# Storing the first chunk's x^T earlier, and transposing the keys of two more pieces on VectorE

## The chip, the cores and the metric

The kernel runs on one core of a Trainium2 chip. The core has five engines with a queue of instructions each: TensorE (matrix products; PE in the profile, its weight loads PEld), VectorE (DVE), ScalarE (ACT), GpSimd (POOL) and SyncE (SP), which here issues nearly all DMAs. All transfers share 16 DMA engines. The metric is the device time of one execution in microseconds; of several executions the median counts.

## The reference

A causal linear attention with decay (8 batches, 8 heads, 576 tokens, head size 64), whose output is laid out as 4608 tokens by 512 features, and then a two-layer network with an activation of its own:

```python
gamma = 1.0 - 2.0 ** (-5.0 - np.arange(H))
Dmat = np.where(rel >= 0, gamma[:, None, None] ** rel[None, :, :], 0.0)   # rel = i - j
attn = np.matmul(scale * np.matmul(q, k.transpose(0, 1, 3, 2)) * Dmat, v)
x = attn.transpose(0, 2, 1, 3).reshape(B * S, H * D)      # 4608 x 512
h = x @ w_in                                              # 512 x 2048
g = h * erf(softplus(h))
out = g @ w_out                                           # 2048 x 512
```

Everything is float32.

## The kernel before

**Attention by pieces.** The tokens are cut into 36 pieces of 128 tokens, 9 to a pair of batches: four of the first batch, four of the second, and one that holds the last 64 tokens of both. Pieces are counted from 0 here, so the eleventh and twelfth are pieces 10 and 11. Four pieces make a chunk of 512 tokens, nine chunks in all. Of each piece three stages are run, in an order that the list `stages` (L430 to L435) fixes:

- `transposes(i)` (L311) brings queries and keys into the layout with the head dimension on partitions (tiles qT and kT).
- `scores(i)` (L337) multiplies kT and qT (16 products at L343 into two PSUM tiles s), and VectorE masks them into sT (L348, recorded at the helper's line L99).
- `outputs(i)` (L350) multiplies sT with the values (L361) and the running state with qT (L372), adds k^T v of the piece to the state (L384, and L423 for the decay), and VectorE scales the result into the chunk's x^T (`scaled`, recorded at L99). At its end it loads keys and values of piece i + 3 and, from piece 7 on, has GpSimd weigh the values of piece i + 1 (`weigh_values`, L309).

There are two ways to transpose. For an early piece the rows are loaded as they are (`load_rows`, L136, issues at L145); TensorE transposes them against an identity into PSUM (L328: pt_q, pt_k, four blocks of 128x128 each) and ScalarE copies the result out (L330, L334). For a late piece `load_squares` (L123, issues at L131) loads them in another arrangement, four DMAs of 112 KB for a whole piece, and VectorE transposes squares of 32 by 32 straight into qT or kT (L322). Queries go the second way from piece 8 on (`SQUARES`), keys from piece 12 on (`SQUARES_K`), for the pieces that lie in one batch and for the shared ones alike. Keys that come as squares are loaded as rows as well where a piece lies in one batch, because L384 needs them so. Rows have four buffers for k and v; squares have two for qs and two for ks. `transposes(i)` asks for the queries of piece i + 2 at its end, and with them for the square keys.

**The network by blocks.** The hidden features are cut into four groups g; a block is one group and one chunk. Both products use a scheme with seven products of half size for eight, so blocks need sums of weights and of x^T. `First` makes h of a block (L492), the activation follows (L555 to L569), `Second` the block's share of the output (L600). Block (0, 0) and (0, 1) use plain products instead (`plain`, L535, products at L546). For the groups after the first, x^T is read back from the DRAM tile xd, in which `store_x(c)` (L460) puts it: 1 MB for a chunk, one DMA at L461. Chunk 0 is needed from xd only when group 1 begins.

**The order.** It is written out by hand. TensorE, VectorE and the others run their own instructions strictly in the order of the program. Attention is woven in between the products: up to the first block's activation the string at L723 says step by step what is issued (L723 to L739). Its letters: `a` one stage of the attention, `p` one step of the plain products, `s` the store of chunk 0, `w` a load of weights, `c` the second part of the constants, `k` idle products, a digit that many steps of rounding the weights (L250 to L271, on ScalarE, VectorE and GpSimd). After the string come the store of chunk 1 (L744) and the plain products of block (0, 1).

SyncE's queue issues in the program's order as well. The eight semaphores of its DMAs are used in turn, so each DMA waits until the one eight places before it has landed, besides the waits for its buffer.

Of the kernel before, what the change touches and what calls it, by code (L numbers as in the profile page):

```python
# [54 lines left out]
def kernel(  # L55
# [56 lines left out]
    PC = TCH // P  # L112
# [4 lines left out]


    SQUARES = 2 * PC
    SQUARES_K = 3 * PC  # L120
    SQ = 32

    def load_squares(i, name, src):  # L123
        t = raw.tile([P, NP, P * D // SQ], FP32, tag=name + "s", name=f"raw_{name}s", bufs=2)
        for b, s0, n, r0 in pieces[i]:
            m = n // SQ * D
            for part in range(P // SQ):
                e, d0 = part // 2, part % 2 * SQ
                tokens = src[b, e * NP : (e + 1) * NP, s0 : s0 + n, :].rearrange("p (r a) d -> r p (a d)", r=SQ)
                at = r0 // SQ * D  # L130
                nc.sync.dma_start(  # L131
                    out=t[part * SQ : (part + 1) * SQ, :, at : at + m - SQ], in_=tokens[:, :, d0 : d0 + m - SQ]
                )
        return t

    def load_rows(i, name, src, bufs):  # L136
        if name == "q":
            t = raw.tile([P, NP, P * D // SQ], FP32, tag="qs", name="raw_q", bufs=bufs)
            t = t.rearrange("p a x -> p (a x)")[:, : H * D].rearrange("p (h d) -> p h d", h=H)
        else:  # L140
            t = raw.tile([P, H, D], FP32, tag=name, name=f"raw_{name}", bufs=bufs)
        for b, s0, n, r0 in pieces[i]:
            for e in range(2):
                heads = src[b, e * NP : (e + 1) * NP, s0 : s0 + n, :]
                nc.sync.dma_start(out=t[r0 : r0 + n, e::2, :], in_=heads.rearrange("h p d -> p h d"))  # L145
        return t

    def load(i, names="qkv"):
        if i < len(pieces):
            t = loaded.setdefault(i, {})  # L150
            for name in names:
                src = {"q": q, "k": k, "v": v}[name]
                if name == "q" and i < SQUARES:
                    t["q"] = load_rows(i, "q", q, 2)
                elif name == "q":
                    t["qs"] = load_squares(i, "q", q)
                    if i >= SQUARES_K:
                        t["ks"] = load_squares(i, "k", k)
                elif name == "v" or i < SQUARES_K or len(pieces[i]) == 1:
                    t[name] = load_rows(i, name, src, 4)  # L160
# [67 lines left out]
    def load_weights():  # L228
        part = next(coming, None)
        if part is not None:  # L230
            t = wraw.tile([P, 2 * WP], UINT32, tag="wraw", name="wraw")
            for rows, src in part[0]:
                nc.sync.dma_start(out=t[rows].rearrange("p (h f) -> p h f", h=2), in_=src)
            words.append((t, *part[1:]))
# [49 lines left out]
    def round_weights(n=1):  # L284
        for _ in range(n):
            next(round_step, None)
# [159 lines left out]
    def attend(upto):  # L446
        while done[0] < min(upto, len(stages)):
            of, i = stages[done[0]]
            of(i)
            done[0] += 1  # L450
# [9 lines left out]
    def store_x(c):  # L460
        nc.sync.dma_start(out=xd[c], in_=x[0, c][:, :n_dc])  # L461
# [242 lines left out]
    def keep_busy(n):  # L704
        for _ in range(n):
            nc.tensor.matmul(idle[:, :P], lhsT=ident, rhs=ident, start=True, stop=True)
# [13 lines left out]

    for what in "alkakakawkakakawaa3awwa2aaa5ppappawwppa5ppapp5wawcppa5ppappaa5s":  # L723
        if what == "a":
            attend(done[0] + 1)
        elif what == "p":
            next(products)
        elif what == "s":
            store_x(0)
        elif what == "l":  # L730
            load(2, "kv")
        elif what == "c":
            nc.sync.dma_start(out=cst[:, CONST_FIRST:], in_=consts[:, CONST_FIRST:])
        elif what == "w":
            load_weights()
        elif what == "k":
            keep_busy(2)
        else:
            round_weights(int(what))  # L739
# [92 lines left out]
```

## Time and profile before

| | |
|---|---|
| median of 5 runs | 1028.24 us (1026.79 to 1029.47) |
| the profiled execution's own time | 1028.24 us |
| its span on the core | 1026.5 us |
| TensorE busy | 1017.3 us (99%), 6346 products |
| VectorE busy | 668.6 us (65%) |
| ScalarE busy | 390.6 us (38%) |
| GpSimd busy | 122.6 us (12%) |
| DMA | 165.76 MB, 161 GB/s on average |
| SyncE's loads of queries as squares, L131 | 96 of 112 KB, 4.5 us to landing |
| SyncE's loads of keys as squares, L131 | 84 of 112 KB, 4.2 us to landing |
| stores of x^T, L461 | 9 of 1 MB, 5.3 us to landing |
| transposition of kT on VectorE, L322 | 27, 1102 ns at the median |
| transposition of keys on TensorE, L328 | 48 blocks of 128x128, 12 copies of 588 ns on ScalarE |

Busy time is the union of an engine's instructions; TensorE's products overlap, so the duration of one (272 ns for a block of a transposition) is longer than the step from one to the next. The chain of work is the view that gives each piece of time to one engine, followed back from the last instruction. Times on the axis are microseconds from the start of the span.

### The profile page before, as it was taken

How to read it: one execution, taken by the hardware profiler on the slowest of the kernel's cores; microseconds unless marked ns; L12 is line 12 of the kernel's file. 1: busy time of each engine (PE TensorE's matmuls, PEld its weight loads, DVE VectorE, ACT ScalarE, POOL GpSimd, SP SyncE). 2: the span in 40 equal slices, each digit the busy share in tenths (PEclk: the TensorE clock that was granted, in tenths of full speed). 3: DMA queues.
4: the chain of work that ended last, by engine and by line, in shares of the span. 5: the costliest groups of instructions: out<-in, count | busy, mean ns of one | idle time of the engine just before them, and what ended most of it. 6: DMA issues, size and time to landing. Idle time of an engine off the chain costs nothing.

```text
span 1026.5 us, 15946 instructions
## 1 busy us (share of the span) xinstructions
PE 1017.3 (99%) x6346; PEld 876.4 (85%) x6346; DVE 668.6 (65%) x1054; ACT 390.6 (38%) x481; POOL 122.6 (12%) x122
## 2 busy tenths in 40 slices
PE   9999999999999999999999999999999999999998
PEld 8778888888788888888888888888888888888887
DVE  3868777877976656656666666666567655555555
ACT  2354134233234444434343344444433333333332
POOL 2243112122312110010001001000100000000000
PEclk9999999999999999999999999999999999999999
DMA  9998989979974344544445345444433334444433
GB/s 194 205 247 175 224 194 228 248 149 251 241 179 165 125 145 146 168 161 160 156 147 170 123 146 157 167 146 144 144 124 124 123 131 126 131 136 133 124 92 114
DMA packets 146986, 165.76 MB, mean 161 GB/s; under 512 B 97376, under 2 KB 121568, under 8 KB 138848
## 3 DMA queue, kind: packets, MB, share of 16 engines
q1 hardware_dynamic: 145904, 163.96, 56.6%
q8 instruction: 50, 0.82, 0.3%
q10 hardware_dynamic: 1008, 0.79, 0.3%
q14 instruction: 24, 0.20, 0.1%
HBM read 117.52 MB, written 47.19 MB: 160 GB/s over the span
## 4 chain that ended last, share of the span: by engine, by line
PE 94%; SPq 2%; DMA 2%; DVE 1%; issue 1%; POOL 0%; POOLq 0%; DVEq 0%
PE a L600 24%; PE a L492 23%; PE g L600 12%; PE g L492 12%; PE e L600 6%; PE e L492 6%; PE s L343 3%; PE o L361 3%; DMA raw_v<-in_v_dram 2%; PE o L384 1%; PE o L372 1%; SPq L145 1%; PE p L546 1%; PE pg L546 1%; PE pe L546 1%
## 5 line engine op out<-in xcount | busy, mean ns | idle before, releaser
L492 PE MATMUL a<-x,wa 128*128 128x256 f32 x1088 | 258.3, 380 | 0.0
L492 PEld LDWEIGHTS a<-x,wa 128*128 128x128 f32 x1088 | 205.7, 190 | 28.5
L600 PE MATMUL a<-wb,s 128*128 128x256 f32 x864 | 205.7, 381 | 0.0
L600 PEld LDWEIGHTS a<-wb,s 128*128 128x128 f32 x864 | 162.9, 190 | 23.6 <-ACT o L614 0.7
L99 DVE TENSOR_TENSOR t<-g,t 128x512 f32<-128x512 f32 x68 | 46.9, 690 | 150.3 <-ACT t L522 113.1
L492 PE MATMUL g<-x,wa 128*128 128x256 f32 x544 | 129.2, 380 | 0.0
L492 PEld LDWEIGHTS g<-x,wa 128*128 128x128 f32 x544 | 102.8, 190 | 14.4
L99 DVE TENSOR_TENSOR o<-a,o 128x512 f32<-128x512 f32 x108 | 74.2, 687 | 49.3 <-PE a L600 49.3
L517 ACT COPY t<-a 128x512 f32<-128x512 f32 x34 | 19.9, 586 | 188.2 <-PE a L492 188.2
L99 DVE TENSOR_TENSOR t<-t,s 128x1024 f32<-128x1024 f32 x72 | 88.6, 1271 | 0.0
L561 ACT ACTIVATE s<-t 128x1024 f32<-128x1024 f32 x72 | 72.1, 1048 | 27.6 <-DVE t L99 27.6
L270 POOL TENSOR_TENSOR wraw<-wraw 128x512 f32<-128x512 f32 x28 | 29.4, 1051 | 437.7 <-DVE wraw L268 185.7
L99 DVE TENSOR_TENSOR x<-x 128x512 f32<-128x512 f32 x115 | 75.8, 693 | 1.2
L528 ACT COPY t<-a 128x512 f32<-128x512 f32 x34 | 19.9, 587 | 144.3 <-PE a L492 144.3
L565 ACT ACTIVATE s<-s 128x1024 f32<-128x1024 f32 x72 | 72.1, 1049 | 0.4
L600 PE MATMUL g<-wb,s 128*128 128x256 f32 x288 | 68.6, 381 | 0.0
L600 PE MATMUL e<-wb,t 128*128 128x256 f32 x288 | 68.5, 380 | 0.0
L600 PE MATMUL a<-wb,t 128*128 128x256 f32 x288 | 68.5, 380 | 0.0
L600 PE MATMUL g<-wb,t 128*128 128x256 f32 x288 | 68.2, 380 | 0.0
L99 DVE TENSOR_TENSOR sT<-s,cst 128x512 f32<-128x512 f32 x72 | 46.1, 681 | 32.6 <-PE s L343 32.6
L99 DVE TENSOR_TENSOR o<-g,o 128x512 f32<-128x512 f32 x72 | 49.3, 685 | 24.8 <-ACT o L614 20.0
L492 PE MATMUL e<-x,wa 128*128 128x256 f32 x272 | 64.8, 381 | 0.0
(75 smaller groups left out, 1226.5 us busy)
## 6 DMA issues: line engine op xcount, KB each, us to landing
od<-o SPq DMA_DIRECT2D x54, 512.0 KB, 3.4
x<-xd SPq DMA_DIRECT2D x27, 1024.0 KB, 4.8
o<-od SPq DMA_DIRECT2D x27, 1024.0 KB, 5.6
raw_qs<-in_q_dram SPq DMA_DIRECT2D x96, 112.0 KB, 4.5
raw_ks<-in_k_dram SPq DMA_DIRECT2D x84, 112.0 KB, 4.2
xd<-x SPq DMA_DIRECT2D x9, 1024.0 KB, 5.3
raw_k<-in_k_dram SPq DMA_DIRECT2D x64, 128.0 KB, 4.5
raw_v<-in_v_dram SPq DMA_DIRECT2D x64, 128.0 KB, 4.4
```

Source lines behind the costliest of these rows:

```text
L99: nc.vector.tensor_tensor(out=out, in0=in0, in1=in1, op=op)
L145: nc.sync.dma_start(out=t[r0 : r0 + n, e::2, :], in_=heads.rearrange("h p d -> p h d"))
L270: engine.tensor_tensor(out=r_f, in0=high_f, in1=r_f, op=ALU.mult)
L343: nc.tensor.matmul(ps[e][:, p, :], lhsT=t["kT"][heads[e], p, :], rhs=t["qT"][heads[e], p, :], start=True, stop=True)
L361: nc.tensor.matmul(o[p % 2][heads[(e + p) % 2], p // 2, :], lhsT=t["v"][:, 2 * p + e, :], rhs=t["sT"][:, e, p, :], start=(p < 2), stop=(no ...
L492: nc.tensor.matmul(acc[:, j * TH : (j + 1) * TH], lhsT=weights["wa", self.g][:, a, d, j * P : (j + 1) * P], rhs=x[self.g, self.c][a][:, d, :],
L517: nc.scalar.copy(out=self.t1[:, 1], in_=self.a)
L528: nc.scalar.copy(out=self.t2[:, 0], in_=self.a)
L546: nc.tensor.matmul(acc[n][:, j * TH : (j + 1) * TH], lhsT=wa[:, slots[f], dc % 2, j * P : (j + 1) * P], rhs=t[:, dc, tok * TH : (tok + 1) ...
L561: nc.scalar.activation(self.s[:, j], t, AF.Softplus)
L565: nc.scalar.activation(self.s[:, j], self.s[:, j], AF.Erf)
L600: nc.tensor.matmul(acc[:, tp, :], lhsT=left[:, j * TH + tp * P : j * TH + (tp + 1) * P], rhs=weights["wb", self.g][:, b, j, :], start=(sta ...
```

## The change

Two edits. `SQUARES_K` goes from 12 to 10: the keys of pieces 10 and 11 are loaded as squares too (eight more DMAs; the rows are still loaded) and transposed by VectorE (two more instructions at L322), in place of eight transpositions on TensorE and two copies on ScalarE. And the letter `s` of the string moves from its end to the front of its last stretch: the store of chunk 0 is issued before four steps of products, three stages of attention and five steps of rounding instead of after them. In SyncE's queue it thereby moves ahead of the transfers that these three stages issue: the queries of piece 9 (four DMAs at L131), its keys (two at L145) and its values (two at L145). Later in the queue, the four DMAs of square keys of piece 10 come right behind the square queries of piece 10, and those of piece 11 behind the queries of piece 11.

```diff
-    SQUARES_K = 3 * PC
+    SQUARES_K = 3 * PC - 2
...
-    for what in "alkakakawkakakawaa3awwa2aaa5ppappawwppa5ppapp5wawcppa5ppappaa5s":
+    for what in "alkakakawkakakawaa3awwa2aaa5ppappawwppa5ppapp5wawcppa5sppappaa5":
```

The instructions of GpSimd stay the same, in the same order.

## The prediction

> **What bounds the kernel now.** The first view is the table of stretches, around the place that the diff touches (the store of the first x^T and the transposes of two pieces lie between 57 and 90 us).
>
> ```profile
> core 0: us, PE busy (x) PEld busy (x) DVE busy (x) ACT busy (x) POOL busy (x), PEclk, DMA share, GB/s
> 60.00:80.00 20.00, 20.00 (x206) 16.50 (x204) 14.97 (x29) 8.04 (x12) 7.28 (x7) 1.00 1.08 250
> 80.00:100.00 20.00, 20.00 (x205) 16.36 (x202) 16.86 (x28) 10.59 (x13) 5.71 (x5) 1.00 0.77 170
> 100.00:110.00 10.00, 10.00 (x94) 8.15 (x94) 9.93 (x14) 1.17 (x2) 2.06 (x2) 1.00 0.93 256
> ```
>
> TensorE has no idle time here, and the list of waits shows one real wait of it after 60 us (0.6 us, for kT near 272). So whatever leaves or enters TensorE's own order moves the end one for one. Two other resources are nearly full: the DMA engines at 60 to 80 us (share 1.08) and VectorE at 80 to 110 us.
>
> The second view is the chain that ended last, 66 to 87 us. It runs on TensorE alone and prices what the change removes.
>
> ```profile
> 66.34 1.06 PE pg L546 x4
> 67.41 0.86 PE p L546 x4
> 68.27 0.44 PE pt_k L328 x4
> 68.71 0.86 PE p L546 x4
> ...
> 76.16 0.86 PE pe L546 x4
> 77.02 0.44 PE pt_k L328 x4
> 77.46 0.87 PE pg L546 x4
> ...
> 84.75 1.73 PE a L600 x8
> 86.48 0.44 PE pt_k L328 x4
> 86.92 1.73 PE e L600 x8
> ```
>
> The blocks at 77.02 and 86.48 are the keys of pieces 10 and 11, counted from 0: the two that move to VectorE. The block at 68.27 is piece 9, which stays.
>
> The third view is SyncE's queue, in order of time.
>
> ```profile
> 56.76 0.43 SPq L733 DMA_DIRECT2D cst<-in_decays_dram  x1
> 57.28 2.62 SPq L131 DMA_DIRECT2D raw_qs<-in_q_dram  x4
> 59.95 0.98 SPq L145 DMA_DIRECT2D raw_k<-in_k_dram  x2
> 61.57 1.61 SPq L145 DMA_DIRECT2D raw_v<-in_v_dram  x2
> 63.31 1.13 SPq L461 DMA_DIRECT2D xd<-x  x1
> ```
>
> The qs, k and v here belong to piece 9. From issue to landing the view by tile gives 5.4 us for k, 4.0 for the second v and 6.1 for the 1 MB store: k lands at 60.4 + 5.4 = 65.8, v at 62.8 + 4.0 = 66.8, the store at 63.3 + 6.1 = 69.4. They land in the order of issue, the store 2.6 us behind v.
>
> The fourth is VectorE's timeline around piece 11.
>
> ```profile
> 91.60 2.44 DVE L99 TENSOR_TENSOR wa<-wa 128x512 f32<-128x512 f32 x2
> 93.97 1.27 DVE L99 TENSOR_TENSOR sT<-s,cst 128x512 f32<-128x512 f32 x2
> 95.16 0.69 DVE L322 STREAM_TRANSPOSE qT<-raw_qs 128x512 f32<-128x512 f32 x1
> 95.79 1.11 DVE L322 STREAM_TRANSPOSE kT<-raw_ks 128x512 f32<-128x512 f32 x1
> 98.20 0.69 DVE L99 TENSOR_TENSOR o<-g,o 128x512 f32<-128x512 f32 x1 [1.31 <-ACT o L614]
> ```
>
> sT of piece 11 is ready at 95.24; TensorE uses it at 97.48 (L361). That is 2.24 us of cover. From sT of piece 9 at 75.13 to the end of kT at 96.90 VectorE idles once, 1.17 us at 83 to 84.18, and that for GpSimd's wb, which itself waited for VectorE's L268. So whatever is inserted after 75.13 arrives undiminished at 93.97.
>
> **What the Trainium skill says.** "DMA: Bandwidth & Descriptors", Queues, rings and completion order: each DMA engine consumes its descriptors in ring order. The landings above agree (65.8, 66.8, 69.4), so a store that is issued earlier pushes back all that now comes behind it. "TensorEngine Tiling (Array Packing)", Key Properties: a change of tiling mode drains TensorE. The trace agrees: eight products take 1.92 us right after a group with 64-row weights and 1.73 otherwise; both removed blocks stand between full-size products, so no drain goes with them. "SBUF — State Buffer", SBUF: two separate sides: a VectorE instruction with two SBUF inputs and a GpSimd one exclude each other. The pair wa at 91.60 took 2.44 us beside GpSimd's weighing of v (92.00, 1.49 us), the pair at 88.65 took 1.37.
>
> **The change, part by part.**
>
> *Removed from TensorE:* 2 x 4 transposes, 2 x 0.44 = 0.88 us, on the path, nothing hides it. Gain 0.88. With them go two copies of 0.59 us on ScalarE, which idled 7.1 us before the first: worth nothing. Two fewer PSUM tiles of "at" are taken; the four then turn as they do from piece 12 on, where TensorE never waits for one: nothing.
>
> *Store moved.* It now stands behind the constants (56.76), ahead of three transfers of piece 9: four issues of qs, two of k, two of v. It depends on nothing late (its x^T is complete after piece 3), so it goes at about 57.3. Everything behind it slides by its transfer, 2.6 us by the landings. k of piece 9: 65.8 + 2.6 = 68.4. TensorE begins to load it as weights at 67.89, and with the 0.13 us that GpSimd took between v's landing (66.84) and its start (66.97) the load begins at 68.55. This is a new wait of 0.66 us in front of everything on TensorE. The cover was 67.89 - 65.84 = 2.05 us, which is just too little. Bounds: 0 if engines that were idle behind v at 63 to 65 us take the store faster; 1.75 if it costs 3.6 us, the stretch in which the 1 MB passed (64.3 to 68, at 200 to 370 GB/s). By conservation it can't be much worse, since the same bytes were through at 69.4 before. I take 0.66. qs of piece 9 lands at 65.0 + 2.6 = 67.6, used on VectorE at 68.22: hidden. v lands near 69.5 instead of 66.8, so GpSimd's weighing starts 2.6 us later; GpSimd has nothing else until 73.38 and TensorE needs v at 79.12: hidden. From k of piece 10 on, the bytes ahead are the same as before: no change.
>
> *Added transfers.* Eight DMAs of 112 KB, about 0.55 us apart by their kind's landings: 4.4 us. The square keys of piece 10 take the places in the queue that the square queries of piece 11 hold now, the last of which is issued at 75.03 and lands at 79.6. VectorE wants them after qT, at 80.24: covered by 0.6 us, and by 0.9 more until TensorE would wait (it needs kT at 82.5 - 0.44 = 82.1, so the keys at 81.1; an earlier wait of TensorE adds to this). All behind them slides by 2.2, then 4.4 us: square keys of piece 11 about 84 (needed 89.7), k and v of piece 11 from 81.4 to 86 (needed 92.0), queries and keys of piece 12 by 90 (needed 95.2). The DMA engines are free at 80 to 82 and 83 to 84 us, so the slide is gone by about 92. Eight more issues of 0.43 us on SyncE lie in the same wait. All hidden: nothing.
>
> *Added on VectorE:* two transpositions of kT at 1.08 to 1.14 us each, of which 0.92 (124.39 to 125.31) to 1.11 counts because instructions overlap: 1.0 each. The first stands ahead of L263 and L268, so wb on GpSimd and VectorE's wait for it slide with it. s of piece 10 needs kT at 82.1 and gets it at 81.3 (plus the same 0.66 both): hidden. With the second, sT of piece 11 ends at 95.24 + 2.0 = 97.24, while TensorE would arrive at 97.48 - 0.88 = 96.60; the 0.66 us shift both. The wait is 0.6 us (0.2 of it already at piece 10: 87.9 against 87.7). Bounds: 0 if wa at 91.6 no longer meets GpSimd and gets back 1.07 us; 0.95 at 1.13 each. After that VectorE is led again by TensorE's outputs at 99.24: sT of piece 12 ended at 105.42 and was used at 106.38, so the lag left over, up to 0.4 us, fits: nothing more.
>
> *Sum:* -0.88 + 0.66 + 0.6 = +0.4 us. The profiled execution took 1028.24 us (span 1026.5 and 1.7 around it), which is the median of the five runs too (1026.79 to 1029.47). Forecast 1028.6, 0.04% slower; by the 0.2% (2.06 us) that a measurement of this kernel tells from none, no change.
>
> **Rivals.**
>
> *The gain arrives, 1027.0.* k lands in time and VectorE gets its port back: -0.88. If also the wait of 0.6 us near 272 closes, -1.5: 1026.7. For it: the two lower bounds are possible. Against: the queue is full exactly where the store goes in. To be faster by over 2.06 us it would need more idle time than TensorE has after 57 us, so this rival, too, stays inside 0.2%, apart from the spread of runs.
>
> *k of piece 9 comes much later, 1031.0.* The store would have to cost k over 4.4 us, a landing after 70.2: its stragglers (the constants landed 6.0 us after their issue, most of their packets long before) would hold back k by the store's 3.6 us and a late second issue of k, which waits for the landing of the weights issued at 56.34 (61.5). With 3.0 us of wait: -0.88 + 3.0 + 0.6 = +2.7. It decides from a wait of 2.35 us on. Against: 69.4, when the same bytes were through.
>
> *VectorE becomes the bound to 110 us, 1030.3.* 9.93 of 10 us are busy at 100 to 110. Without any cover, 2.2 + 0.66 - 0.88 = +2.0, at the very edge. Against: the idle 1.31 + 0.34 us at 97 to 99.
>
> *The square keys of piece 10 come late, 1031.* They would have to land after 81.1 (81.8 with the 0.66) instead of 79.6; each us past that costs one, 2 us late gives 1030.6, 2.4 gives 1031.0. For it: they are asked for only at 73 to 75, in the fullest stretch. Against: in the same place of the queue other rows of the same size landed at 79.6.
>
> **How the numbers follow.** The sum near zero, with both waits between their bounds: 0.52, and the gain in full: 0.20, both within 0.2% but for 0.08 (spread of runs and what I didn't see) that I give to faster and 0.02 to slower. k much later 0.10, VectorE as the bound 0.09, square keys late 0.09, of which 0.10 together end inside the 0.2% and 0.18 beyond it. So faster 0.08, within 0.2% 0.72, slower 0.20. The range, 1026.6 to 1031.0, takes in the gain in full and the late k; beyond it I leave 0.08 below and 0.10 above.
>
> **What would show it.** Right: pt_k only up to 68.5 us, eight transposes fewer; a wait of TensorE for raw_k there, 0.3 to 1.2 us; the store issued at 57.3 and landed near 65.5; kT from raw_ks 29 times, the first near 81; no wait for raw_ks longer than 0.5 us; a wait of o (L361) for sT near 97, about half a us. Wrong: TensorE idle over 2 us in one place between 68 and 110, or no wait at all and the span shorter by 0.9.

## The result, and the profile after

| | before | after |
|---|---|---|
| median | 1028.24 us, 49 runs | 1029.53 us, 28 runs |
| lowest and highest | 1026.79, 1029.82 | 1026.90, 1033.49 |
| the profiled execution, its span | 1028.24, 1026.5 us | 1029.54, 1027.8 us |

The ratio of the times is 1.0015, with a 95% interval of 1.0009 to 1.0020: the change costs 1.5 us (0.9 to 2.1). The means of the runs lie 1.5 us apart, the medians 1.3. That is within 0.2% and inside the range, on the side that the forecast named, but 1.1 us more than its +0.4. The highest run moved up by 3.7 us, the lowest hardly at all.

The table of stretches after the change, with one short stretch more (the columns are those of before):

```profile
core 0: us, PE busy (x) PEld busy (x) DVE busy (x) ACT busy (x) POOL busy (x), PEclk, DMA share, GB/s
60.00:80.00 20.00, 19.06 (x190) 15.34 (x187) 14.52 (x26) 6.96 (x10) 8.07 (x7) 1.00 1.13 278
80.00:100.00 20.00, 20.00 (x205) 16.26 (x201) 18.75 (x30) 10.12 (x13) 5.71 (x5) 1.00 1.04 200
100.00:110.00 10.00, 10.00 (x95) 8.19 (x94) 9.93 (x14) 1.17 (x2) 2.06 (x2) 1.00 0.90 249
66.00:70.00 4.00, 3.06 (x16) 2.46 (x16) 3.94 (x7) 0.61 (x2) 0.07 (x1) 1.00 1.35 212
```

TensorE, without a gap here before, now lacks 0.94 us, all of it at 66 to 70. VectorE has 1.9 us more at 80 to 100 (18.75 for 16.86), the two transpositions. The DMA share at 80 to 100 went from 0.77 to 1.04.

The chain that ended last, 63 to 87 us:

```profile
63.66 4.93 DMA raw_k<-in_k_dram
68.59 0.14 issue
68.73 0.63 PE pt_k L328 x4
69.36 0.86 PE p L546 x4
...
76.81 0.86 PE pe L546 x4
77.67 0.86 PE pg L546 x4
...
84.97 1.73 PE a L600 x8
86.69 1.73 PE e L600 x8
```

It no longer runs on TensorE alone. It comes from the keys of piece 9, issued at 63.66 and landed at 68.59; TensorE follows 0.14 us later. Between pe and pg, and between a and e, the two blocks of transposes are gone.

SyncE's queue:

```profile
56.61 1.72 SPq L233 DMA_DIRECT2D wraw<-in_moe_w_out_dram  x1
58.38 0.43 SPq L733 DMA_DIRECT2D cst<-in_decays_dram  x1
58.86 0.43 SPq L461 DMA_DIRECT2D xd<-x  x1
59.38 3.69 SPq L131 DMA_DIRECT2D raw_qs<-in_q_dram  x4
63.12 1.21 SPq L145 DMA_DIRECT2D raw_k<-in_k_dram  x2
64.43 1.24 SPq L145 DMA_DIRECT2D raw_v<-in_v_dram  x2
```

The store stands behind the constants and ahead of piece 9, as planned. But the constants themselves are issued at 58.38, not at 56.76, because the load of weights in front of them held the queue for 1.72 us in this execution, and for 0.38 before.

VectorE's timeline around piece 11:

```profile
94.06 2.44 DVE L99 TENSOR_TENSOR wa<-wa 128x512 f32<-128x512 f32 x2
96.42 1.28 DVE L99 TENSOR_TENSOR sT<-s,cst 128x512 f32<-128x512 f32 x2
97.62 0.70 DVE L322 STREAM_TRANSPOSE qT<-raw_qs 128x512 f32<-128x512 f32 x1
98.25 1.07 DVE L322 STREAM_TRANSPOSE kT<-raw_ks 128x512 f32<-128x512 f32 x1
```

sT comes 2.45 us later than before (96.42 for 93.97). The idle time of 1.31 us in front of the next instruction is used up, and wa still takes 2.44 us. TensorE pays for it in the products of sT (TensorE's timeline, the outputs of pieces 10 and 11), before:

```profile
88.58 1.09 PE L361 MATMUL o<-sT,raw_v 128*64 128x128 f32 x16
...
97.48 1.09 PE L361 MATMUL o<-sT,raw_v 128*64 128x128 f32 x16
```

and after:

```profile
88.35 1.26 PE L361 MATMUL o<-sT,raw_v 128*64 128x128 f32 x16
...
97.42 1.42 PE L361 MATMUL o<-sT,raw_v 128*64 128x128 f32 x16
```

The group of 16 products took 1.09 us for either piece; it now takes 1.26 for piece 10 and 1.42 for piece 11. It is stretched rather than preceded by an idle time: that of piece 11 starts at 97.42, when the second of the two instructions that write sT has not ended.

Last, TensorE's lines in the list of waits (total, times, longest, in us), before:

```profile
PE s L343 <- DVE kT L322: 0.6, 1, 0.6
PE pt_k L328 <- DMA raw_k<-in_k_dram: 0.2, 1, 0.2
```

and after:

```profile
PE s L343 <- DVE kT L322: 1.6, 2, 0.9
PE pt_k L328 <- DMA raw_k<-in_k_dram: 1.5, 2, 0.9
```

The second line holds the predicted wait, its longest, 0.94 us; the other 0.5 us lie ahead of 20 us. In the first there is one that was not predicted, at 234.78 (timeline of VectorE and TensorE); the other, near 273, was there before:

```profile
233.53 1.10 DVE L322 STREAM_TRANSPOSE kT<-raw_ks 128x512 f32<-128x512 f32 x1 [1.38 <-DMA raw_ks<-in_k_dram]
...
234.78 1.16 PE L343 MATMUL s<-qT,kT 64*128 64x128 f32 x16 [0.94 <-DVE kT L322]
```

If each TensorE instruction's start is subtracted from that of the same instruction before, the difference is -0.48 us from 33 us on (waits of the start-up that were shorter in this execution), +0.65 behind the wait at 68, +0.21 and -0.22 behind the two removed blocks, -0.06 and +0.27 behind the outputs of pieces 10 and 11, and +1.3 from 235 us to the end. The spans differ by 1.3. So two questions were left: what does the store cost, and does the wait at 234 belong to the added transfers?

### The profile page after: what moved, and what is told of

Its sections match the earlier page's. It is cut to its first block, busy times and chain, and to the rows that moved or that the text cites. A ratio compares the mean times of both kernels' runs of the same rounds, so it can differ in the third digit from the quotient of the medians.

```text
span 1027.8 us, 15940 instructions
## 1 busy us (share of the span) xinstructions
PE 1016.6 (99%) x6338; PEld 875.0 (85%) x6338; DVE 672.5 (65%) x1056; ACT 389.5 (38%) x479; POOL 124.0 (12%) x122
## 4 chain that ended last, share of the span: by engine, by line
PE 88%; DMA 5%; SPq 2%; DVE 2%; POOL 1%; ACT 1%; issue 1%; DVEq 0%; POOLq 0%
PE a L600 23%; PE a L492 22%; PE g L600 12%; PE g L492 11%; PE e L600 6%; PE e L492 5%; PE s L343 2%; PE o L361 2%; DMA raw_v<-in_v_dram 2%; DMA raw_ks<-in_k_dram 1%; DMA wraw<-in_moe_w_in_dram 1%; PE o L384 1%; PE o L372 1%; SPq L131 1%; SPq L145 1%; PE p L546 1%
```

## The experiments

All ratios are to the kernel before, timed beside them on the same chip. Not all rows come from one chip, so the ratios are to be compared, not the medians.

| kernel | median us | ratio, 95% interval |
|---|---|---|
| store moved only | 1028.65 | 1.0015 (1.0008 to 1.0023) |
| keys only, store at its old place | 1028.04 | 1.0005 (0.9997 to 1.0013) |
| added transfers only, unread | 1028.95 | 1.0010 (1.0002 to 1.0018) |
| change, store still earlier | 1027.98 | 1.0005 (0.9997 to 1.0013) |
| change, store behind the keys of piece 9 | 1028.44 | 1.0009 (1.0002 to 1.0015) |
| added transpositions on VectorE only | 1027.72 | 1.0002 (0.9993 to 1.0010) |
| keys without added transfers | 1027.84 | 0.9998 (0.9990 to 1.0007) |
| TensorE's part only | 1026.85 | 0.9993 (0.9986 to 0.9999) |
| square keys of piece 11 only | 1027.18 | 0.9995 (0.9987 to 1.0003) |

**The store alone.** Only the letter `s` moves.

```diff
-    for what in "alkakakawkakakawaa3awwa2aaa5ppappawwppa5ppapp5wawcppa5ppappaa5s":
+    for what in "alkakakawkakakawaa3awwa2aaa5ppappawwppa5ppapp5wawcppa5sppappaa5":
```

> Only the store moves; the keys of pieces 10 and 11 stay with TensorE. Theory (the store holds back the keys of piece 9, and nothing else of the change costs more than it gives): TensorE waits about 1 us for raw_k at 68 to 69 us, no later wait is new, all that follows is 0.7 to 1.1 us later than before: ratio 1.0007 to 1.0011. Rival (the store is hidden, all the loss is from the keys): no wait for raw_k near 68, ratio 1.000.

It costs 1.5 us (0.8 to 2.4), as much as the whole change and more than the 0.7 to 1.1 expected. TensorE's timeline:

```profile
69.68 0.63 PE L328 MATMUL pt_k<-ident,raw_k 128*128 128x128 f32 x4 [1.43 <-DMA raw_k<-in_k_dram]
```

The wait is there without the key edit, and longer than in the changed kernel. Behind it TensorE is 1.61 us later than before, and it was level in front of it.

**The keys alone.**

```diff
-    SQUARES_K = 3 * PC
+    SQUARES_K = 3 * PC - 2
```

> Only the keys of pieces 10 and 11 move to VectorE; the store stays behind the transfers of piece 9. Theory: no wait for raw_k at 68; TensorE is 0.88 us ahead after 87 us, gives back 0.6 us in waits for sT at 88 and 97 and stands 0.3 us ahead at 100 us. Then two ways: if the eight added transfers keep the queue late until 230 us, TensorE waits about 1 us there for kT and the ratio is 1.0005 to 1.001; if that late wait in the changed kernel's profile was chance, the ratio is 0.9995 to 1.000. Rival (the store is not the cause, the keys are all of it): ratio 1.0015.

+0.5 us (-0.3 to 1.3), no measurable difference. In its profile TensorE gains 0.44 us at each of the two blocks that are gone and gives back 0.28 at 89.6 and 0.32 at 98.5; there is no wait near 68 or 233.

**The key edit taken apart.** Three kernels: only the added DMAs, whose data nobody reads; only two transpositions more on VectorE, into a tile that nobody reads; and the move from TensorE to VectorE without the DMAs, the keys of pieces 10 and 11 being transposed from the squares of the queries.

```diff
 # added transfers only
+                    elif i >= SQUARES_K - 2:
+                        load_squares(i, "k", k)
 # transpositions only
+        if i in (10, 11):
+            extra = att.tile([P, NP, P], FP32, tag="extra", name="extra", bufs=1)
+            squares = t["qs"].rearrange("p h (a d) -> p h a d", d=D)
+            nc.vector.transpose(out=extra.rearrange("p h (r a) -> p h a r", r=SQ), in_=squares[:, :, :, :SQ])
 # without added transfers
+            if i in (10, 11) and name == "k":
+                t["ks"] = t["qs"]
```

> The kernel before, with the square keys of pieces 10 and 11 loaded in their place of the queue but read by nobody: eight more DMAs of 112 KB, no instruction of another engine differs. If added bytes keep the queue late up to 230 us, the loads stand 1 to 1.5 us later there and TensorE waits 0.5 to 1.0 us for kT near 233: ratio 1.0005 to 1.001. If the queue catches up at 125 to 140 us, where it is half idle, no wait of TensorE is new and the ratio is 1.000.

> The kernel before with one more transposition on VectorE at piece 10 and one at piece 11, of data that are there anyway and into a tile that nobody reads; TensorE keeps its own transpositions, and no transfer is added. Theory (the two cost only where TensorE has been moved ahead of them): sT of piece 11 ends near 97.2 instead of 95.2 and TensorE uses it at 97.5: no wait, ratio 1.000, at most 1.0003. Rival (VectorE is the bound up to 110 us): 1 to 2 us of waits between 88 and 111 us, ratio 1.001 to 1.002.

> Keys of pieces 10 and 11 as in the change, transposed by VectorE and not by TensorE, but out of the square queries that are there anyway: no transfer is added, and the store stays where it was (the keys of these two pieces are thereby wrong values). It is the keys' half of the change without its eight DMAs. Theory: TensorE 0.88 us ahead at 87 us, 0.3 us ahead at 100 us after two waits for sT, and nothing new later: ratio 0.9997, range 0.999 to 1.0002; the difference to the same with the transfers (1.0005) is theirs. Rival (the transfers cost nothing, the loss lies in VectorE's order): ratio as with the transfers, 1.0005.

Transfers that nobody reads cost 1.0 us (0.2 to 1.8). By SyncE's queue, landings are 4.4 us later than before at 86 us and still 3.0 at 111; the slide is down to 0.4 only at 133. (Of this, 1.1 us were there at 77, ahead of the first added transfer. In a second execution, shown below, landings were 0.65 us sooner than before at 77, 3.9 later at 87 and 0.9 later at 111.) TensorE's loss in this profiled execution lies at 233 to 273 (two waits for kT, 1.1 us in sum, and a late sT).

The transpositions alone cost nothing that shows (+0.2 us, -0.7 to +1.0). Timelines of VectorE and TensorE (the added lines make L361 L365):

```profile
96.01 1.27 DVE L99 TENSOR_TENSOR sT<-s,cst 128x512 f32<-128x512 f32 x2
...
97.65 1.09 PE L365 MATMUL o<-sT,raw_v 128*64 128x128 f32 x16
```

sT ends at 97.28; TensorE comes at 97.65 and its group keeps the 1.09 us. With TensorE's own transposes still there, the cover of 2.24 us holds the 2.0. Without them and without the DMAs (the third kernel) the group takes 1.41 us again, and TensorE gives back 0.19 at 89 and 0.32 at 98; the time is that of the kernel before (-0.2 us, -1.0 to +0.7). So VectorE's price is paid only because TensorE arrives 0.88 sooner.

**TensorE's part alone.** The transposition of the keys of pieces 10 and 11 is left out on all engines; their scores use kT of piece 9.

```diff
+            if i in (10, 11) and name == "k":
+                t["kT"] = nine[0]
+                continue
...
+            if i == 9 and name == "k":
+                nine.append(tT)
```

> The kernel before with the eight transpositions of the keys of pieces 10 and 11 and their two copies left out; these pieces take kT of piece 9, so no work replaces them. It is the gain of the change by itself. Theory (what leaves TensorE's order moves the end one for one): TensorE stands 0.44 us ahead from 77 us and 0.88 us from 87 us on, no wait for sT at 88 and 97, ratio 0.9991. Rival (later waits, for transfers or for VectorE between 230 and 275 us, take the gain back): ratio 0.9995 to 1.000, with the lead gone behind such a wait.

-0.7 us (-1.4 to -0.1). In the profile TensorE gains 0.43 and 0.44 at the two places and no wait follows. The predicted gain is real and arrives at the end when nothing else is added.

**The store at other places.** Both kernels contain the key edit; in the first the store goes in front of the queries of piece 8, in the second between the keys and the values of piece 9.

```diff
 # still earlier
+    for what in "alkakakawkakakawaa3awwa2aaa5ppappawwppa5ppapp5wsawcppa5ppappaa5":
 # behind the keys of piece 9
-        load(i + 3, "kv")
+        load(i + 3, "k")
+        if i == 6:
+            store_x(0)
+        load(i + 3, "v")
```

> The changed kernel with the store of chunk 0 a stretch earlier still, ahead of the square queries of piece 8 (near 52 us instead of 59), where the DMA engines are half idle (share 0.45 to 0.6 at 50 to 52 us). Theory: part of the store's 2.6 us falls into that idle time, the keys of piece 9 land near 67 and TensorE waits 0 to 0.4 us for them instead of 0.9; against the changed kernel 0.6 to 1.1 us are gained: ratio to before 1.0003 to 1.001. Rival (the store costs the same wherever it stands ahead of piece 9): ratio as the changed kernel's, 1.0015.

> The changed kernel with the store of chunk 0 between the keys and the values of piece 9: the same DMAs, the store one place (two DMAs of values) earlier than in the kernel before, and the values of piece 9 alone behind it. Theory (the store costs by making the keys of piece 9 late, and only by that): no wait for raw_k near 68, TensorE's lead at 77 and 87 us as with the keys' half alone, the values later by 2 to 3 us without a wait of TensorE; ratio 1.0005, as the keys' half alone, 0.001 below the changed kernel. Rival (the store costs by its bytes in a full stretch, wherever it stands ahead): some of the wait stays, ratio 1.001 to 1.0015.

The first is at +0.5 us (-0.3 to 1.3), the value of the key edit alone, with a wait of 0.33 us left on TensorE, as the theory had it; the interval overlaps that of the change, so a gain over it is not shown. In the second the wait is gone (TensorE's timeline):

```profile
67.61 0.60 PE L328 MATMUL pt_k<-ident,raw_k 128*128 128x128 f32 x4
```

Yet its time, +0.9 us (0.2 to 1.5), is not shown to be better than that of the change: the intervals overlap, and it lies between what the theory and the rival gave. Its profiled execution was 1.4 us faster than its median, so what held up the others is not in that trace.

**Half of the keys.** Only piece 11 goes to VectorE.

```diff
-    SQUARES_K = 3 * PC
+    SQUARES_K = 3 * PC - 1
```

> The keys of piece 11 alone move to VectorE, with four more DMAs; the store stays where it was. A half of the change that could beat both kernels: TensorE gains 0.44 us, sT of piece 11 ends at 96.2 when TensorE arrives at 97.0, so that nothing is given back there; half the added transfers. Theory: ratio 0.9995 to 1.0002, as the late waits for transfers grow by half of what eight DMAs cost. Rival (they grow with any added transfer): 1.0005.

-0.5 us (-1.3 to +0.3): the lowest of the versions that leave nothing out, but not distinguished from the kernel before.

**Second executions.** Does the wait after 230 us belong to a kernel, or to one execution of it? The change, the added transfers alone and the kernel before once more, unaltered, one execution each (1028.77, 1027.12 and 1027.88 us).

> The change itself in a second execution, to see which of its waits belong to it. Theory: the wait for raw_k of piece 9 near 68 us comes back, 0.5 to 1.7 us, because the store's transfer in front of those keys is there in every execution; and TensorE waits again between 230 and 275 us, for kT or sT that came late through the transfers, 0.5 us or more in sum. Rival: the waits of the first profiled execution after 230 us were that execution's own; then TensorE loses less than 0.3 us there, and the span is 1.0 us shorter than the first one's 1027.8.

> The kernel before with the square keys of pieces 10 and 11 loaded and left unread, a second execution. Theory: the added transfers cost by waits of TensorE at 230 to 275 us, in sum 1.0 us more than in the kernel before (1.5 in the first profiled execution against 0.6). Rival: the place and size vary so much from one execution to the next that no wait after 230 us is the loads' own: then the sum is within 0.3 us of the kernel before's 0.6.

> The kernel before in a second execution. Theory: no wait of TensorE near 68 us over 0.3 us, none at 230 to 240, and at most the 0.6 us for kT near 272. Rival: it too shows waits of 0.5 us or more at 230 to 268 us, and then those of the changed kernel say little.

The chain of the change in its second execution:

```profile
64.47 5.07 DMA raw_k<-in_k_dram
69.55 0.14 issue
69.68 0.63 PE pt_k L328 x4
```

and its line in the list of waits:

```profile
PE pt_k L328 <- DMA raw_k<-in_k_dram: 2.8, 3, 1.8
```

The wait for raw_k is back, with 1.80 us at that place (the other two lie ahead of 33 us). The one after 230 is not: this list has no line for kT from VectorE. The table of stretches for 140 to 275 us says the same of the added transfers, first execution:

```profile
140.00:275.00 135.00, 133.47 (x1287) 108.50 (x1285) 106.73 (x178) 40.23 (x54) 32.45 (x31) 1.00 0.94 220
```

and second:

```profile
140.00:275.00 135.00, 134.97 (x1296) 110.04 (x1295) 109.00 (x182) 40.05 (x53) 33.77 (x33) 1.00 0.98 224
```

TensorE lacks 1.53 us in the one and 0.03 in the other. The kernel before lacked 0.62 and then 0.89. Of the seven executions with all the added transfers, this stretch lacks 1.59, 0, 0, 0, 0.29, 1.53 and 0.03 us; of the six without any, 0.62, 0.89, 0, 0, 0.32 and 0 (and the one with half of them 1.05). My theory for this place has fallen: those waits come and go in either kind. The wait near 68 is another matter. TensorE's weight loads of that block, before and after (view of PEld, where the time in front of an instruction stands in brackets):

```profile
67.89 0.57 PEld L328 LDWEIGHTS pt_k<-ident,raw_k 128*128 128x128 f32 x4
```

```profile
68.70 0.42 PEld L328 LDWEIGHTS pt_k<-ident,raw_k 128*128 128x128 f32 x4 [1.31 <-issue]
```

The second DMA of piece 9's keys, in eight executions:

| execution | issued | landed | TensorE ready | its weight load waited |
|---|---|---|---|---|
| before | 60.43 | 65.84 | 67.89 | 0 |
| before, second | 60.97 | 66.42 | 67.13 | 0 |
| keys only | 61.30 | 65.82 | 67.42 | 0 |
| change, store behind these keys | 60.58 | 65.13 | 67.40 | 0 |
| change, store still earlier | 63.46 | 67.97 | 67.38 | 0.70 |
| change | 63.66 | 68.59 | 67.39 | 1.31 |
| store only | 64.33 | 69.55 | 67.85 | 1.80 |
| change, second | 64.47 | 69.55 | 67.48 | 2.17 |

In all four traces with the store ahead of these keys TensorE waits, and in none of the ten others (six of them not in the table, with landings at 65.0 to 66.7).

## Why the prediction was right or wrong

*"Removed from TensorE: 0.88".* Right. The part alone measured -0.7 us (-1.4 to -0.1), and its profile shows 0.43 + 0.44.

*"VectorE: the wait is 0.6 us (0.2 of it already at piece 10)".* Right within 0.1 us: 0.17 at piece 10 and 0.33 at piece 11 in the changed kernel, 0.18 and 0.32 in its second execution. That wa might get back 1.07 us did not happen. "Nothing more" after that holds too; no traced execution of the change shows an idle TensorE from there to 110 us.

*"Store moved: 65.8 + 2.6 = 68.4 ... a new wait of 0.66 us".* The mechanism is right, the size is the term that failed. In the first profile the landing was nearly exact (68.59), and TensorE's position after it as well (+0.65), but that is luck: TensorE had come there 0.48 us sooner than before, and the wait swallowed it. Counted from where TensorE stood in front of it, the step cost 1.13, 1.62 (store only) and 2.00 us (second execution), 1.6 on average, and the last is above my upper bound of 1.75. The store's own share, 2.6 us, was right: it landed 2.64, 2.63 and 2.63 us behind the constants. What failed are the two ends, both taken from one execution. The keys' landing without the store (65.84) rests on constants that landed at 62.80; in the other two executions with the store they landed at 63.53 and 63.48, and the six transfers from the store to the keys took 3.31 to 3.44 us, where from the constants to the keys they had taken 3.04 (2.99 to 3.58 in the ten executions with the keys ahead). So the keys came 2.2 to 3.7 us later than in the two executions before. And TensorE was ready at 67.13 to 68.06 in the fourteen executions traced, so that 67.89 was one of its later times; in these three it was 67.39 to 67.85. I also let the store go at "about 57.3", right behind constants issued at 56.76; it went at 58.86 to 59.67. In the first execution this cost nothing, since its constants landed at 62.64 all the same.

The Trainium skill's "DMA: Bandwidth & Descriptors", Queues, rings and completion order, which the step rested on, agrees with these runs: the store landed at 65.28 and the keys behind it at 67.99 and 68.59, in order.

*The sum.* -0.88 + 1.6 + 0.5 = +1.2 us, against +1.5 (0.9 to 2.1). The store's term alone is enough for the miss; that the added transfers cost something besides is not excluded.

*"Added transfers: all hidden, nothing ... the slide is gone by about 92".* Right for every consumer that I named: the square keys of piece 10 landed at 80.1 and kT began at 80.82. The second half is wrong: landings are still 1.8 us late at 112 and at 127, after 0.8 at 77, ahead of the added ones. The price is not settled. Transfers alone measured +1.0 us (0.2 to 1.8); with and without them the key edit measured +0.5 and -0.2, intervals that overlap. No place could be shown where such a cost is always paid.

*The rivals.* "k much later" was the near one. It asked for a wait from 2.35 us on, and the second execution had 2.17; runs of up to 1033.49 us (1032.63 for the store alone, and never over 1029.82 before) would fit longer ones, but none of those was traced. There is another candidate for them. All eight runs over 1031 us of these two kernels have a mean granted TensorE clock of 0.998, and of their other runs only one is below 0.999 (1030.84 us, 0.997). Of a time of 1030 us, 0.001 is 1.0 us, by my estimate what such a step of the clock costs. Without these nine runs both kernels are on average 0.9 us above the kernel before, not 1.5. Whether a longer wait brings the lower clock stays open. (The keys alone had one run of 1031.51 us, with a clock of 1.000.) VectorE as the bound and late square keys did not occur. The gain in full came only with TensorE's part alone.

*What would show it.* Store issued "at 57.3": 58.86; landed "near 65.5": 65.28. kT from raw_ks 29 times, the first "near 81": 29, at 80.82. A wait for raw_k of "0.3 to 1.2": 0.94, then 1.80. For sT near 97, "about half a us": 0.33. VectorE did wait more than 0.5 us for raw_ks (1.38 at 233.53), which I had said it would not; at the same place it had waited 1.22 before.

## What to carry to other kernels

Price a DMA that is moved forward by every transfer that it overtakes, and take the cover of each (landing to use) from several executions: 2 us of cover in one trace was 0.7 in the next, and a store of 1 MB in front used up all of it in each of four traces. A wait that one trace shows far behind the change should be looked for in a second execution of both kernels before it is explained. Work moved off the engine that sets the end is worth its time only up to the cover of the engine that takes it over: here 0.5 of the 0.88 us were given back.

## What the runs showed of the hardware

The same DMA in SyncE's queue, the constants, was issued at 56.55 to 59.19 us in executions whose queue is the same up to there. In the ten executions with piece 9's keys ahead of the store, a late start shows in their landing only in part: seven with constants issued at 56.55 to 57.30 had the keys at 65.02 to 65.84, three with constants at 58.10 to 58.84 had them at 65.82 to 66.69, on average 1.6 us later in the issue and 0.9 in the landing. With the store right behind the constants, the keys landed at 68.59 where these were issued at 58.38, and at 69.55 where they were issued at 59.16 and 59.19, 0.8 us later in the issue and 1.0 in the landing. So the queue seems to make up for part of a late start, and less of it with 1 MB put in; three executions are too few to show the latter. The second surprise is how much one kernel's TensorE differs far from any edit: 1.53 and 0.03 us of waiting between 140 and 275 us in two executions whose spans are 1028.0 and 1025.3 us.
